# A retention layer and two feed-forward layers on one core: the first block's x made chunk by chunk from PSUM, weight tiles converted one step further ahead, weight loads issued ahead of the stores

## The chip, the core and the metric

The kernel runs on one core of a Trainium2 chip. The metric is the device time of one execution in microseconds (us). Before the change the median of three runs is 888.38 us (887.61 to 889.36). The engines are called as in the profile: PE is TensorE's matrix products (PEld its weight loads), DVE is VectorE, ACT is ScalarE, POOL is GpSimd, SP is the queue that issues most DMAs.

## What is computed

Retention over 4 batches, 8 heads, 576 positions, head size 64, then two feed-forward layers with 2304 tokens, model width 512 and inner width 2048. The weights arrive as 64-bit floats.

```python
scores = (q @ k.T) / sqrt(64)
ret    = scores * Dmat            # gamma_h ** (i - j) for i >= j, else 0
x      = (ret @ v)                # regrouped to 2304 x 512
h = x @ w_in;  x = max(0.01*h, h) @ w_out      # layer 0, leaky
h = x @ w_in2; x = (h * cos(h)) @ w_out2       # layer 1
```

## The kernel before

**Tiles.** The 2304 tokens are 18 chunks of 128 for the retention, and five blocks of 512, 512, 512, 384 and 384 for the feed-forward layers. The inner width is cut into 16 pieces f, so a layer has 5 x 16 steps (block, f) and both layers 160. The retention of chunk i gives the x of 128 tokens; block 0 needs chunks 0 to 3, and these are worked through before the first step. The later chunks are laid between the steps.

**Precision.** Every operand of the feed-forward products is held as a high and a low half (`hi` rounded to fp32r, `lo` the rest), and a product is three fp32r products. So x, the hidden g and the weights w are each split by ACT (the high half) and DVE (the low half: a subtraction). One step has 12 products into the inner width (`h_mm`, L393) and 12 out of it (`o_mm`, L407).

**Weights.** A piece of the weights, here called a grain, comes in as 64-bit words by a DMA (`load_raw`, `load_half`), and is turned into fp32 by `conv_a` (ACT, L307 and L308), `conv_b` (DVE, L313, L315 and L319), `conv_c` (DVE, L326), `conv_d` (ACT, L335, the high half) and `conv_e` (DVE, L338, the low half). The main program calls them as `ready`, `conv_b`, `add_of`, `high_of` and `low_of`. Layer 0's grains are converted while the 16 steps of block 0 run; layer 1's are converted later in halves, each stored to DRAM (`stash`) and fetched again.

**The first x.** For chunk i, `scores` (L166), `masks` (L182), `values` (L197, L211), `states` (L231) and `reads` (L244) leave the chunk's output in two banks of PSUM, and `take` (L270, four ACT instructions of 128x128, one for each of the four groups of heads) scales it into `xr`. Once all four chunks of block 0 are there, `split_x(0)` cuts the four tiles of 128x512 into halves (ACT L379, DVE L380).

**Order.** The schedule is written out by hand: each engine runs its instructions in the order in which the program issues them, and a semaphore wait at the head of an engine's queue holds all behind it. The first part is a list of calls (L572 to L635), then a loop over the steps. In step s of block 0, DVE converts grain s + 2 and makes the low half of grain s + 1, with the low half of g and the work of a later chunk between. SP's DMA issues are in program order too. Before the first chunk the program issues 16 products of zeros (`warm`, L280).

Of the kernel before, what the change touches and what calls it, by code (L numbers as in the profile page):

```python
# [7 lines left out]
F32 = mybir.dt.float32  # L8
F32R = mybir.dt.float32r
# [4 lines left out]
ALU = mybir.AluOpType  # L14
# [5 lines left out]
P = 128  # L20
# [48 lines left out]
def retention_ffn_ffn(  # L69
# [29 lines left out]
        tabs_sb[:, sum(sizes[:x]) : sum(sizes[: x + 1])] for x in range(4)  # L99
    )  # L100

    zero = xp.tile([P, 2 * T], F32, tag="x", name="zero")[:, :P]
    one = const.tile([P, 1], F32, name="one")
    psum = psp.tile([P, 8, 512], F32, name="psum")

# [31 lines left out]
    def scale_v(i):  # L137
        c = i % CYCLE * H
        if i in (1, 2) or n_first <= i < n_busy:
            for h in range(H):  # L140
                v = ch_t[i][:, 3, h * D : (h + 1) * D]
                nc.scalar.activation(v, v, AF.Copy, scale=vtab_sb[:, c + h : c + h + 1])
            return
        v3 = ch_t[i][:, 3].rearrange("p (h d) -> p h d", h=H)
        t3 = vtab_sb[:, c : c + H].unsqueeze(2).to_broadcast([P, H, D])
        eng = nc.gpsimd if i else nc.vector
        eng.tensor_tensor(out=v3, in0=v3, in1=t3, op=ALU.mult)
# [111 lines left out]
    def take(i):  # L259
        b = banks_of(i)  # L260
        j = max(j for j in range(NB) if T0[j] <= i * P)
        t0 = i * P - T0[j]
        c = i % CYCLE
        parts = ((0, 1, c), (1, 2, CYCLE)) if c == CROSS else ((0, 2, c),)
        for p in range(NP):
            if t0 == 0:
                xr[j, p] = xrp.tile([P, T], F32, tag="xr", name="xr")
            o = NP * C + p * C
            for x0, x1, t in parts:
                nc.scalar.activation(  # L270
                    xr[j, p][:, t0 + x0 * C : t0 + x1 * C].rearrange("p (x c) -> p x c", c=C),
                    psum[:, b + x0 : b + x1, o : o + C],
                    AF.Copy,
                    scale=otab_sb[:, t * NP + p : t * NP + p + 1],
                )


    def warm(n, bank):
        for _ in range(n):
            nc.tensor.matmul(psum[:, bank, :P], zero, zero, start=True, stop=True)  # L280

# [39 lines left out]
    def conv_c(g):  # L323
        lo, _ = words(g)
        i = t_t[g].bitcast(I32)
        nc.vector.tensor_tensor(out=i, in0=i, in1=lo.bitcast(I32), op=ALU.add)  # L326
        raw_t.pop(g)
# [18 lines left out]
    def stash_w(g):  # L346
        t = t_t.pop(g)
        both = rawp_t[g].rearrange("p (a n) -> p a n", a=2).bitcast(F32R)
        nc.scalar.copy(both[:, 1], t)  # L349
        nc.gpsimd.tensor_tensor(  # L350
            out=both[:, 0], in0=t, in1=both[:, 1].bitcast(F32), op=ALU.subtract
        )
        nc.sync.dma_start(w2[g[1]][g[2]], rawp_t.pop(g).rearrange("p (a n) -> p a n", a=2))


    def fetch_w(f):
# [148 lines left out]
    def next_half():  # L505
        if half_n[0] < len(half_q):
            load_half(*half_q[half_n[0]])
            half_n[0] += 1
# [7 lines left out]
    def add_of(k):  # L516
        if k < len(grains):
            conv_c(grains[k])
            if grains[k][2] is not None:
                next_half()  # L520
            elif k in after:
                load_raw(after[k])

    def high_of(k):
        if k < len(grains):
            if not grains[k][2]:
                new_w(0, grains[k][1])
            conv_d(grains[k])

    def low_of(k):  # L530
        if k < len(grains):
            conv_e(grains[k], nc.vector)

    def ready(k):
        if k < len(grains):
            conv_a(grains[k])
# [25 lines left out]
    def stash(s):  # L562
        for g in stash_at.get(s - 1, ()):
            conv_b(g)
            conv_c(g)
            stash_w(g)
            next_half()
        for g in stash_at.get(s, ()):
            conv_a(g)

    with tc.manual_schedule():
        nc.scalar.dma_start(tabs_sb, tabs)  # L572
        nc.vector.memset(zero, 0.0)

        nc.scalar.copy(one, zero[:, :1])
        load_chunk(0)
        load_raw(0)
        for i in range(1, n_first):
            load_chunk(i)
        for f in range(1, 4):  # L580
            load_raw(f)
        scale_q(0)
        scale_v(0)
        warm(WARM[0], 3)
        scores(0)
        masks(0)
        ready(0)
        values(0)
        scale_v(1)
        conv_b(grains[0], lambda: scale_q(1))  # L590
        scores(1)
        masks(1)
        values(1)
        scale_v(2)
        states(0)
        reads(0)
        take(0)
        scale_q(2)
        scores(2)
        add_of(0)  # L600
        high_of(0)
        scale_q(3)
        scores(3)
        masks(2)
        ready(1)
        scale_v(3)
        values(2)
        low_of(0)
        masks(3)
        states(1)  # L610
        reads(1)
        take(1)
        values(3)

        def second():
            states(2)

        conv_b(grains[1], second)
        reads(2)
        take(2)  # L620
        states(3)
        reads(3)
        take(3)
        load_chunk(4)
        load_raw(4)
        load_chunk(5)
        for f in range(5, 10):
            load_raw(f)
        for _ in range(2):
            next_half()  # L630
        add_of(1)
        split_x(0)
        high_of(1)
        low_of(1)
        ready(2)  # L635

        for s in range(len(steps) + LAG[1]):
            lj, f = steps[s] if s < len(steps) else (None, None)
            i = chunk_at.get(s)
            if lj is not None:  # L640
                nxt = lj + 1 if lj + 1 < 2 * NB else None
                if s == last:
                    early.close()
                    fp = ctx.enter_context(tc.tile_pool(name="fp", bufs=2))
                if f == 2 and nxt is not None and nxt >= NB:
                    load_x(nxt)
                h_mm(lj, f)
                if f == NF - 1 and nxt is not None and nxt < NB:
                    split_x(nxt)
                if i is not None:  # L650
                    values(i)
                if s + 1 in chunk_at:
                    scores(chunk_at[s + 1])
            prev = steps[s - 1] if 1 <= s <= len(steps) else None
            if lj is not None and lj < NB:
                leaky(lj, f)
                if s < NF:

                    def between():
                        if s:  # L660
                            low_of(s + 1)
                        if s in (1, 2):
                            g_low(*prev)

                    if s + 2 < len(grains):
                        conv_b(grains[s + 2], between)
                    else:
                        between()
                    add_of(s + 2)
                    ready(s + 3)  # L670
                    high_of(s + 2)
                g_high(lj, f)
            if i is not None:
                states(i)
            if s + 1 in chunk_at:
                masks(chunk_at[s + 1])
            if n_first <= chunk_at.get(s + 2, 0) < n_busy:
                scale_q(chunk_at[s + 2])
                scale_v(chunk_at[s + 2])
            if prev and prev[0] < NB and prev in graw:  # L680
                g_low(*prev)
            for q in outs.get(s, ()):
                o_mm(*q)
            if i is not None:
                reads(i)
                take(i)
                if i + 2 < NCH:
                    load_chunk(i + 2)
                    if i + 2 >= n_busy:
                        scale_q(i + 2)  # L690
                        scale_v(i + 2)
            for q in outs.get(s, ()):
                if q[1] == NF - 1:
                    if lj is not None and lj < NB:

                        g_low(lj, f)
                    evacuate(q[0])
            if lj is not None and lj >= NB:
                cos_a(lj, f)
            if prev and prev[0] >= NB:  # L700
                cos_c(*prev)
            if lj is not None and lj >= NB:
                cos_b(lj, f)
            if prev and prev[0] >= NB:
                g_low(*prev)
            stash(s)
            for qj, qf in outs.get(s - 1, ()):
                if qj == NB - 1:
                    fetch_w(qf)
# [49 lines left out]
```

## Time and profile before

| | before |
|---|---|
| median of three runs | 888.38 us |
| the profiled execution's own time | 888.93 us |
| its span (first to last instruction) | 887.1 us |
| busy in the span: PE, DVE, ACT, POOL | 863.2, 575.2, 398.1, 71.2 us |
| mean granted TensorE clock | 0.988 |
| moved by DMA | 110.88 MB |

The 1.8 us between the span and the execution's own time lie around the first and the last instruction. Busy time of a row is the sum over its instructions; a bracket at a row's end gives how long the engine had stood idle before it and what ended that. [...]

### The profile page before, as it was taken

What the parts mean: (1) busy time and instruction counts of PE and PEld (TensorE: products, weight loads), DVE (VectorE), ACT (ScalarE), POOL (GpSimd) and SP (SyncE); (2) the same over time, 40 slices, a digit from 0 to 9 for tenths busy, and PEclk for the clock granted to TensorE, in tenths of its full rate; (3) what the DMA queues carried; (4) which work ended last, traced back from release to release, by engine and by line L of the source; (5) the groups of instructions that cost most, each with busy time, mean ns of one, the idle gap of its engine ahead of it and who ended that gap; (6) DMA issues with size and microseconds to landing.
All of it is one profiled execution on the core that took longest, in us unless ns stands there. A gap on an engine that the chain in (4) does not pass through costs nothing.

```text
span 887.1 us, 14814 instructions
## 1 busy us (share of the span) xinstructions
PE 863.2 (97%) x6048; PEld 753.2 (85%) x6048; DVE 575.2 (65%) x953; ACT 398.1 (45%) x738; POOL 71.2 (8%) x57
## 2 busy tenths in 40 slices
PE   6689999999999999989999999999999999999998
PEld 6568888777887888989999888888888888999998
DVE  5699974343654446554211897777777777888885
ACT  4588764434554446344322343343334333433433
POOL 0000020222212231311000000000000000000000
PEclk8699999999999999999999999999999999999999
DMA  9915522455464546551687700210021002100100
GB/s 361 419 45 198 182 98 83 156 189 168 167 236 144 191 143 215 193 189 71 241 310 261 255 24 1 95 49 1 1 71 48 1 1 72 48 1 1 37 1 35
DMA packets 35860, 110.88 MB, mean 125 GB/s; under 512 B 3408, under 2 KB 8528, under 8 KB 31696
## 3 DMA queue, kind: packets, MB, share of 16 engines
q1 hardware_dynamic: 35648, 109.59, 34.6%
q8 instruction: 47, 0.77, 0.4%
q10 hardware_dynamic: 144, 0.35, 0.1%
q14 instruction: 21, 0.17, 0.1%
HBM read 79.00 MB, written 30.93 MB: 124 GB/s over the span
## 4 chain that ended last, share of the span: by engine, by line
PE 90%; DVE 4%; DMA 3%; ACT 1%; issue 1%; POOL 0%; SPq 0%; DVEq 0%; ACTq 0%; POOLq 0%
PE psum L393 42%; PE psum L407 42%; PE psum L244 2%; DMA raw<-in_w 2%; PE psum L166 1%; PE psum L197 1%; PE psum L211 1%; DVE t L326 1%; DVE t L319 1%; DMA x<-x_hi 1%; ACT t L307 0%; DVE w L338 0%; DVE t L313 0%; DVE g L459 0%; DVE t L315 0%
## 5 line engine op out<-in xcount | busy, mean ns | idle before, releaser
L393 PE MATMUL psum<-x_sb,w 128*128 128x512 f32 (+1 forms) x1920 | 425.3, 370 | 4.8 <-DVE x_sb L380 3.2
L407 PE MATMUL psum<-g,w 128*128 128x512 f32 (+1 forms) x1920 | 424.1, 369 | 0.0
L393 PEld LDWEIGHTS psum<-x_sb,w 128*128 128x128 f32 x1920 | 351.2, 189 | 52.5 <-DVE x_sb L380 3.8
L407 PEld LDWEIGHTS psum<-g,w 128*128 128x128 f32 x1920 | 347.9, 188 | 46.7 <-DVE g L459 0.4
L454 ACT CAST g<-graw 128x512 fp32r<-128x512 f32 (+1 forms) x160 | 92.6, 579 | 221.2 <-DVE graw L483 103.3
L459 DVE TENSOR_TENSOR g<-graw,g 128x512 fp32r<-128x512 f32 (+1 forms) x160 | 103.6, 648 | 86.5 <-ACT g L454 86.3
L477 ACT ACTIVATE r_sb<-r_sb 128x512 f32<-128x512 f32 (+1 forms) x80 | 47.3, 591 | 131.6 <-DVE r_sb L476 131.4
L467 DVE TENSOR_SCALAR t_sb<-psum 128x512 f32<-128x512 f32 (+1 forms) x80 | 51.0, 637 | 63.0 <-PE psum L393 63.0
L445 ACT ACTIVATE graw<-psum 128x512 f32<-128x512 f32 (+1 forms) x80 | 44.2, 553 | 53.6 <-PE psum L393 53.5
L307 ACT ACTIVATE t<-raw 128x512 f32<-128x512 f32 (+1 forms) x49 | 40.1, 819 | 34.4 <-DMA raw<-in_w 32.6
L350 POOL TENSOR_TENSOR t<-t 128x512 fp32r<-128x512 f32 x32 | 43.6, 1368 | 131.1 <-ACT t L349 99.6
L475 DVE SCALAR_TENSOR_TENSOR r_sb<-t_sb,r_sb 128x512 f32<-128x512 f32 (+1 forms) x80 | 51.1, 639 | 2.8
L476 DVE SCALAR_TENSOR_TENSOR r_sb<-t_sb,r_sb 128x512 f32<-128x512 f32 (+1 forms) x80 | 51.1, 639 | 2.7
L474 DVE SCALAR_TENSOR_TENSOR r_sb<-t_sb,psum 128x512 f32<-128x512 f32 (+1 forms) x80 | 50.8, 635 | 2.7
L483 DVE SCALAR_TENSOR_TENSOR graw<-r_sb,psum 128x512 f32<-128x512 f32 (+1 forms) x80 | 50.0, 624 | 1.7 <-ACT r_sb L478 1.7
L478 ACT ACTIVATE r_sb<-r_sb 128x512 f32<-128x512 f32 (+1 forms) x80 | 47.1, 589 | 2.5
L326 DVE CUSTOM_DVE_ANT_0 t<-raw,t 128x1024 uint16<-128x1024 uint16 (+1 forms) x49 | 42.6, 870 | 4.8
L313 DVE TENSOR_SCALAR t<-t 128x512 f32<-128x512 f32 (+1 forms) x49 | 28.1, 574 | 25.6 <-ACT t L307 25.5
L319 DVE SCALAR_TENSOR_TENSOR t<-raw,t 128x512 uint32<-128x512 uint32 (+1 forms) x49 | 42.9, 875 | 1.1
L182 DVE TENSOR_TENSOR p_sb<-psum,tabs_sb 128x512 f32<-128x512 f32 x18 | 12.4, 688 | 47.7 <-PE psum L166 42.6
L308 ACT ACTIVATE raw<-raw 128x512 int32<-128x512 uint32 (+1 forms) x49 | 40.1, 819 | 0.0
L472 DVE TENSOR_SCALAR t_sb<-t_sb 128x512 f32<-128x512 f32 (+1 forms) x80 | 31.5, 393 | 0.0
(35 smaller groups left out, 352.8 us busy)
## 6 DMA issues: line engine op xcount, KB each, us to landing
ch<-in_qkv SPq DMA_DIRECT2D x17, 1024.0 KB, 5.7
raw<-in_w SPq DMA_DIRECT2D x34, 512.0 KB, 5.1
w<-t SPq DMA_DIRECT2D x32, 512.0 KB, 3.0
w<-w SPq DMA_DIRECT2D x32, 512.0 KB, 5.4
raw<-in_w SPq DMA_DIRECT2D x15, 1024.0 KB, 8.8
x_sb<-x SPq DMA_DIRECT2D x12, 512.0 KB, 6.3
x<-x_hi SPq DMA_DIRECT2D x12, 256.0 KB, 2.8
x<-x_lo SPq DMA_DIRECT2D x12, 256.0 KB, 2.9
```

Of the source, the lines that this page charges most:

```text
L319: nc.vector.scalar_tensor_tensor(out=u, in0=hi, scalar=0xC0000000, in1=u, op0=ALU.bitwise_and, op1=ALU.bitwise_or)
L326: nc.vector.tensor_tensor(out=i, in0=i, in1=lo.bitcast(I32), op=ALU.add)
L393: nc.tensor.matmul(hp, wt[:, i ^ hi, ks], x_t[lj, k][:, j, :n], start=(k == 0 and a == 0), stop=(k == KK - 1 and a == 2),)
L407: nc.tensor.matmul(psum[:, BANK_O + m, :n], wt[:, i ^ hi, ms], gt[:, j, :n], start=(f == 0 and a == 0), stop=(f == NF - 1 and a == 2),)
L454: nc.scalar.copy(g_t[lj, f][:, 0, : TB[lj % NB]], g)
L459: nc.vector.tensor_tensor(out=gt[:, 1, :n], in0=graw.pop((lj, f)), in1=gt[:, 0, :n].bitcast(F32), op=ALU.subtract)
L467: nc.vector.tensor_scalar(t, h_t[lj, f], INV_2PI, MAGIC, op0=ALU.mult, op1=ALU.add)
L474: nc.vector.scalar_tensor_tensor(out=r, in0=t, scalar=-C1, in1=hp, op0=ALU.mult, op1=ALU.add)
L475: nc.vector.scalar_tensor_tensor(out=r, in0=t, scalar=-C2, in1=r, op0=ALU.mult, op1=ALU.add)
L476: nc.vector.scalar_tensor_tensor(out=r, in0=t, scalar=-C3, in1=r, op0=ALU.mult, op1=ALU.add)
L477: nc.scalar.activation(r, r, AF.Sin, scale=0.5)
L483: nc.vector.scalar_tensor_tensor(out=g, in0=sq_t.pop((lj, f)), scalar=0.5, in1=h_t.pop((lj, f)), op0=ALU.subtract, op1=ALU.mult,)
```

## The change

Four edits. (1) For block 0 `take` no longer writes `xr`: for each of the four groups of heads ACT writes the high half of the chunk straight from PSUM into the x tile (new L275), and DVE the low half from the same PSUM values (new L276, scale and subtract in one instruction); `split_x(0)` goes. (2) `warm` can issue products of 512 zero columns: two after `values(0)`, two after `reads(3)`; the tile of zeros moves to another buffer. (3) The conversions of block 0 run one grain further ahead: `conv_b` of grains 1 and 2 is issued in the first part, and step s converts grain s + 3 and makes the low half of grain s + 2. (4) In `stash` the next raw load is issued ahead of the store of the grain just converted.

```diff
-    zero = xp.tile([P, 2 * T], F32, tag="x", name="zero")[:, :P]
+    zero = wp.tile([P, T], F32, tag=f"w{NF // 4 - 1}", name="zero")
...
         parts = ((0, 1, c), (1, 2, CYCLE)) if c == CROSS else ((0, 2, c),)
+        if j == 0:
+
+            for p in range(NP):
+                if t0 == 0:
+                    x_t[0, p] = xp.tile([P, 2, T], F32R, tag="x", name="x_sb")
+                hi, lo = (
+                    x_t[0, p][:, e, t0 : t0 + P].rearrange("p (x c) -> p x c", c=C) for e in range(2)
+                )
+                o = NP * C + p * C
+                src, by = psum[:, b : b + 2, o : o + C], otab_sb[:, c * NP + p : c * NP + p + 1]
+                nc.scalar.activation(hi, src, AF.Copy, scale=by)
+                nc.vector.scalar_tensor_tensor(
+                    out=lo, in0=src, scalar=by, in1=hi.bitcast(F32), op0=ALU.mult, op1=ALU.subtract
+                )
+            return
...
-    def warm(n, bank):
+    def warm(n, bank, cols=P):
         for _ in range(n):
-            nc.tensor.matmul(psum[:, bank, :P], zero, zero, start=True, stop=True)
+            nc.tensor.matmul(psum[:, bank, :cols], zero[:, :P], zero[:, :cols], start=True, stop=True)
...
         for g in stash_at.get(s - 1, ()):
             conv_b(g)
             conv_c(g)
+            next_half()
             stash_w(g)
-            next_half()
...
         values(0)
+        warm(2, 1, T)
         scale_v(1)
...
         reads(0)
-        take(0)
         scale_q(2)
         scores(2)
         add_of(0)
+        take(0)
         high_of(0)
...
         reads(1)
+        values(3)
+        conv_b(grains[1], lambda: states(2))
         take(1)
-        values(3)
-
-        def second():
-            states(2)
-
-        conv_b(grains[1], second)
+        ready(2)
         reads(2)
-        take(2)
-        states(3)
+        add_of(1)
+
+        def third():
+            states(3)
+            take(2)
+
+        conv_b(grains[2], third)
+        high_of(1)
         reads(3)
+        warm(2, 7, T)
+        low_of(1)
         take(3)
...
-        add_of(1)
-        split_x(0)
-        high_of(1)
-        low_of(1)
-        ready(2)
+        add_of(2)
+        high_of(2)
+        ready(3)
...
                     def between():
-                        if s:
-                            low_of(s + 1)
                         if s in (1, 2):
                             g_low(*prev)
-
-                    if s + 2 < len(grains):
-                        conv_b(grains[s + 2], between)
+                        low_of(s + 2)
+
+                    if s + 3 < len(grains):
+                        conv_b(grains[s + 3], between)
                     else:
                         between()
-                    add_of(s + 2)
-                    ready(s + 3)
-                    high_of(s + 2)
+                    add_of(s + 3)
+                    ready(s + 4)
+                    high_of(s + 3)
```

What this does to the order on ACT in the first part, from the first `take` to the second (`psum` holds the chunk's output, `w_338` and `w_344` are the first weight tile, `t_` and `raw` the next grain). Before:

```order
L270 ACTIVATE xr<-psum,tabs_sb 128x128 [waits DVE_49,PE_49]
L270 ACTIVATE xr<-psum,tabs_sb 128x128 x3
L335 CAST w_338<-t_195 128x1024 [waits DVE_49]
L307 ACTIVATE t_359<-raw 128x1024 [waits DMAHW7_49]
L308 ACTIVATE raw<-raw 128x1024
```

And now:

```order
L275 ACTIVATE x_sb<-psum,tabs_sb 128x128 [waits DVE_49,PE_49]
L275 ACTIVATE x_sb<-psum,tabs_sb 128x128 [waits DVE_49] x3
L350 CAST w_344<-t_195 128x1024
L322 ACTIVATE t_365<-raw 128x1024 [waits DMAHW7_49]
L323 ACTIVATE raw<-raw 128x1024
```

The second, third and fourth read of a chunk now each wait for DVE, where none waited before.

On DVE, from the third chunk's states to the low half of the third weight tile (`w_565`, now `w_556`; `t_359`, now `t_365`, is grain 1, `t_541`, now `t_471`, is grain 2). Before:

```order
L231 TENSOR_TENSOR st<-psum,st 128x256 [waits DVE_49,PE_49] x2
L326 ISA t_359<-raw,t_359 128x2048 [waits Activation_49]
L380 TENSOR_TENSOR x_sb<-xr,x_sb 128x512 [waits Activation_49] x4
L338 TENSOR_TENSOR w_538<-t_359,w_538 128x1024 [waits Activation_49]
L313 TENSOR_SCALAR t_541<-t_541 128x1024 [waits Activation_49]
L315 TENSOR_SCALAR t_541<-t_541 128x1024 [waits DVE_49]
L319 SCALAR_TENSOR_TENSOR t_541<-raw,t_541 128x1024 [waits DMAHW0_49,DVE_49]
L326 ISA t_541<-raw,t_541 128x2048 [waits DVE_49,Activation_49]
L313 TENSOR_SCALAR t_562<-t_562 128x1024 [waits Activation_49]
L315 TENSOR_SCALAR t_562<-t_562 128x1024 [waits DVE_49]
L338 TENSOR_TENSOR w_565<-t_541,w_565 128x1024 [waits Activation_49]
```

And now:

```order
L231 TENSOR_TENSOR st<-psum,st 128x256 [waits PE_49]
L231 TENSOR_TENSOR st<-psum,st 128x256 [waits DVE_49,PE_49]
L276 SCALAR_TENSOR_TENSOR x_sb<-psum,tabs_sb,x_sb 128x128 [waits Activation_49] x4
L334 SCALAR_TENSOR_TENSOR t_471<-raw,t_471 128x1024 [waits DMAHW0_49]
L353 TENSOR_TENSOR w_506<-t_365,w_506 128x1024 [waits Activation_49]
L276 SCALAR_TENSOR_TENSOR x_sb<-psum,tabs_sb,x_sb 128x128 [waits Activation_49] x4
L341 ISA t_471<-raw,t_471 128x2048 [waits DVE_49]
L328 TENSOR_SCALAR t_558<-t_558 128x1024 [waits DVE_49,Activation_49]
L330 TENSOR_SCALAR t_558<-t_558 128x1024 [waits DVE_49]
L353 TENSOR_TENSOR w_556<-t_471,w_556 128x1024
```

Each chunk's four low halves stand among the conversions, and the last chunk's stand behind the low half of the second weight tile.

On DVE, from the low half of the second step's g (L459, now L475) to the scaling of chunk 4's q (L135), which `scores(4)` on PE waits for. Before, it follows the words of grain 4 (`t_589`):

```order
L459 TENSOR_TENSOR g<-graw,g 128x512 [waits Activation_49]
L319 SCALAR_TENSOR_TENSOR t_589<-raw,t_589 128x1024 [waits DMAHW3_49,DVE_49]
L326 ISA t_589<-raw,t_589 128x2048 [waits DVE_49]
L135 TENSOR_TENSOR ch<-ch,tabs_sb 128x512 [waits DMAHW2_49]
L313 TENSOR_SCALAR t_616<-t_616 128x1024 [waits Activation_49]
```

And now it follows the words of grain 5 (`t_607`):

```order
L475 TENSOR_TENSOR g<-graw,g 128x512 [waits Activation_49]
L353 TENSOR_TENSOR w_610<-t_580,w_610 128x1024
L334 SCALAR_TENSOR_TENSOR t_607<-raw,t_607 128x1024 [waits DMAHW5_49,DVE_49]
L341 ISA t_607<-raw,t_607 128x2048 [waits DVE_49]
L135 TENSOR_TENSOR ch<-ch,tabs_sb 128x512 [waits DMAHW2_49]
L328 TENSOR_SCALAR t_634<-t_634 128x1024 [waits Activation_49]
```

One whole grain more stands ahead of it.

## Rows read from the trace of the kernel before

**Rows 1.** Timeline of PE: start, busy, engine, line, operation, [idle before].

```profile
1.05 6.60 PE L280 MATMUL psum<-zero 128*128 128x128 f32 x32 [1.05 <-DVE zero L573]
...
35.38 8.36 PE L393 MATMUL psum<-x_sb,w 128*128 128x512 f32 x24 [2.48 <-DVE x_sb L380]
...
45.82 2.81 PE L393 MATMUL psum<-x_sb,w 128*128 128x512 f32 x11 [0.76 <-DVE w L338]
48.47 2.88 PE L407 MATMUL psum<-g,w 128*128 128x512 f32 x12
...
54.88 0.69 PE L166 MATMUL psum<-ch 64*64 64x64 f32 x32 [0.81 <-DVE ch L135]
...
66.13 0.68 PE L244 MATMUL psum<-ch,st 64*64 64x64 f32 x16 [0.84 <-DVE st L229]
```

**Rows 2.** Stretches: length, busy us of each engine (instructions), clock, DMA share, GB/s.

```profile
0.00:35.38 35.38, 22.21 (x529) 20.90 (x529) 18.43 (x29) 16.61 (x42) 1.68 (x5) 0.79 0.96 382
35.38:45.82 10.44, 8.86 (x25) 6.52 (x25) 9.39 (x12) 8.51 (x12) 0.00 (x0) 0.73 1.01 418
```

**Rows 3.** Timeline of DVE and ACT in the first part.

```profile
18.59 1.14 ACT L270 ACTIVATE xr<-psum,tabs_sb 128x128 f32<-128x128 f32 x4 [0.44 <-PE psum L244]
18.63 0.69 DVE L135 TENSOR_TENSOR ch<-ch,tabs_sb 128x512 f32<-128x512 f32 x1 [0.54 <-DMA ch<-in_qkv]
...
34.63 2.50 DVE L380 TENSOR_TENSOR x_sb<-xr,x_sb 128x512 fp32r<-128x512 f32 x4 [2.63 <-ACT x_sb L379]
...
44.54 1.23 DVE L338 TENSOR_TENSOR w<-t,w 128x1024 fp32r<-128x1024 f32 x1 [0.54 <-ACT w L335]
```

**Rows 4.** Groups by shape: busy us, mean ns of one | idle before.

```profile
L454 ACT CAST g<-graw 128x512 fp32r<-128x512 f32 x96 | 59.7, 622 | 144.3 <-DVE graw L483 70.6 <-PE psum L407 56.9 <-issue 9.0
...
L270 ACT ACTIVATE xr<-psum,tabs_sb 128x128 f32<-128x128 f32 x64 | 18.3, 369 | 12.8 <-PE psum L244 12.8
...
L307 ACT ACTIVATE t<-raw 128x1024 f32<-128x1024 f32 x15 | 17.2, 1147 | 10.0 <-DMA raw<-in_w 8.2 <-DVE w L338 1.8
...
L335 ACT CAST w<-t 128x1024 fp32r<-128x1024 f32 x15 | 15.8, 1055 | 3.2 <-DVE t L326 3.2
...
L231 DVE TENSOR_TENSOR st<-psum,st 128x256 f32<-128x256 f32 x28 | 11.8, 423 | 27.3 <-PE psum L211 22.8 <-PE psum L244 3.3
...
L573 DVE MEMSET zero<- 128x128 f32 x1 | 0.2, 165 | 0.8 <-PEq L748 0.8
```

**Rows 5.** Timeline of DVE: one grain's conversion while block 0's steps run.

```profile
54.14 0.68 DVE L135 TENSOR_TENSOR ch<-ch,tabs_sb 128x512 f32<-128x512 f32 x1
...
60.80 0.68 DVE L313 TENSOR_SCALAR t<-t 128x1024 f32<-128x1024 f32 x1
...
62.13 1.22 DVE L338 TENSOR_TENSOR w<-t,w 128x1024 fp32r<-128x1024 f32 x1
63.27 1.22 DVE L319 SCALAR_TENSOR_TENSOR t<-raw,t 128x1024 uint32<-128x1024 uint32 x1
64.52 1.23 DVE L326 CUSTOM_DVE_ANT_0 t<-raw,t 128x2048 uint16<-128x2048 uint16 x1
65.66 0.41 DVE L229 COPY st<-psum 128x256 f32<-128x256 f32 x1
66.00 0.68 DVE L459 TENSOR_TENSOR g<-graw,g 128x512 fp32r<-128x512 f32 x1
66.59 0.68 DVE L313 TENSOR_SCALAR t<-t 128x1024 f32<-128x1024 f32 x1
```

**Rows 6.** Timeline of SP, PE and DVE: a raw load and two late waits.

```profile
328.39 0.38 SPq L294 DMA_DIRECT2D raw<-in_w  x1
...
335.56 2.37 PE L393 MATMUL psum<-x_sb,w 128*128 128x384 f32 x12 [0.74 <-DVE x_sb L380]
...
380.66 0.43 DVE L313 TENSOR_SCALAR t<-t 128x512 f32<-128x512 f32 x1 [5.91 <-ACT t L307]
...
384.02 1.15 PE L244 MATMUL psum<-ch,st 64*64 64x64 f32 x32 [3.06 <-DVE st L231]
```

More of the change, by code (lines that the diff above doesn't have):

```diff
@@ L352, in stash_w @@
         )
-        nc.sync.dma_start(w2[g[1]][g[2]], rawp_t.pop(g).rearrange("p (a n) -> p a n", a=2))
+        both = rawp_t.pop(g).rearrange("p (a n) -> p a n", a=2)
+        nc.sync.dma_start(w2[g[1]][g[2]], both)
     def fetch_w(f):
```

## The prediction

> **What bounds the kernel now.** I read the timeline of PE first, since PE is busy 97% of the span and every idle stretch of it is time lost. It stands still for more than half a microsecond at few places [rows 1]: up to 35.38, where the first of block 0's products waits for x; ahead of 45.82, for the low half of the third weight tile; ahead of 54.88, for chunk 4's q, scaled by DVE; ahead of 66.13, for chunk 4's state, also from DVE. After that come only two late waits, 0.74 us at 335.56 and 3.06 at 384.02 [rows 6]. Then I read the stretches [rows 2]: up to 35.38 DVE works 18.43 us of 35.38, from 35.38 to 45.82 it works 9.39 of 10.44. So DVE has room before the first product and none after it. Last I read DVE's own timeline from there [rows 5]: grain after grain without a gap, until PE's backlog hides it from 66.13 on. What the change does to the time is therefore what it does to DVE's arrival at 66.13, and to the two late waits. PE's work after 66.13 is the same in both kernels.
>
> **Prices on DVE** [rows 5], from one start to the next: L313 with L315 1.33 (60.80 to 62.13), L338 1.14, L319 1.25 where L326 follows and 1.14 where something else does, L326 1.14. A grain is thus 4.86 us. A 128x512 operation takes 0.60, a pair of L231 0.85 (two of 423 ns, [rows 4]). From DVE's end to PE's start there is some 0.05 (44.54 + 1.23 to 45.82, [rows 1, 3]); I take this for each handoff between ACT and DVE.
>
> **x from PSUM.** Removed: four ACT casts and four DVE subtractions of 128x512, the latter 2.50 us at 34.63, and the 2.63 that DVE waits ahead of them [rows 3]. Added: 16 small DVE instructions of 128x128 (L276), four a chunk. The order on ACT shows that the second, third and fourth high half of a chunk wait for DVE: the two engines take turns, and DVE waits in line for each turn with all that stands behind it. ACT's half is 369 ns [rows 4], as before. L276 is not in the trace. Above it stands the 128x256 addition from PSUM, 423 ns; below it the 128x128 memset, 165 ns [rows 4]. Length 512 costs 0.68 and 256 costs 0.42, so 128 lies near 0.29, which I take. A pair is 0.37 + 0.29 + 2 x 0.05 = 0.76, and a chunk holds DVE for 3 x 0.76 + 0.2 = 2.5 us even where its first high half is ready.
>
> [...]
>
> **One grain further ahead.** No work is added, but what the engines wait for stands behind one more grain, 4.86 us, as the order on DVE shows for L135. Where DVE has room this is free; I lay DVE's rows in their new order and see where it has none.
>
> Take 0: ACT begins at 18.59 [rows 3], DVE's first half at 19.0, the fourth is through at 21.5. Chunk 3's L135, at 18.63 before, stands behind it: 2.9 us late, and with it PE's scores of chunk 3. Then come L135, two L182, L338, two pairs of L231, L328 with L330, L334: 3 x 0.60 + 1.14 + 2 x 0.85 + 1.33 + 1.14 = 7.1, to 28.6. Take 1 to 31.1; L341 1.14, the next pair of conversions 1.33, chunk 3's states 0.85: 34.4. Take 2 to 36.9; L334 and the second tile's L353, 2.28: 39.2. Now take 3's first half lands: the first product at 39.6 instead of 35.38. Take 3 to 41.7, L341 to 42.95. Here DVE waits: ACT makes the third tile's high half first (1.05) and only then grain 3's words (1.15, [rows 4]), so DVE goes on at 45.2. Two conversions 1.33, the third tile's low half 1.23: 47.8 against 45.77 [rows 3]. PE, ready by about then (24 products took 8.36 us from their start, [rows 1]), is 2.0 late.
>
> Next L334 and L341 follow the low half (started at 46.5): 1.14 + 1.25 + 1.14 = 50.05, L328 and L330 to 51.4, but the first low half of g waits for ACT's high half, behind the fourth tile's: 50.1 + 1.05 + 0.62 [rows 4] = 51.9. The first products out (48.47 before) start at 52.6, 4.1 late. Then 0.60, 1.14, 1.25, 1.14, 1.33 to 57.35, again 0.5 of waiting for ACT, 0.60, and with the fifth tile's low half 1.14, 1.25, 1.14 to 62.0: only here is chunk 4's L135, 0.74 to PE's start. Scores of chunk 4 at 62.75 instead of 54.88: **7.9 us late**. From L135 to L229 DVE has the same kinds of work as before, 11.52 us [rows 5], so 66.13 becomes 74.0, 7.9 late too. After that PE has its backlog, as before.
>
> **Zero products.** [...] They can raise the clock of the first 24 products, whose mean was 0.73 [rows 2], but these end at the third tile's time anyway: worth nothing. The other way, PE now stands idle for nearly 5 us ahead of 62.75, and if its clock falls there, it pays once more what the first 24 products paid at a mean clock of 0.73: 8.36 less twice the 2.88 of the twelve at 48.47 [rows 1], 2.6. The wait of 0.84 that PE had ahead of 66.13 hides that much of it, so 0 to +1.8; I take 0.
>
> **Load ahead of the store.** At 380.66 DVE had waited 5.91 us for ACT, and ACT for a raw load; chunk 13's states stand behind it on DVE, and PE waits 3.06 for them. At 335.56 ACT stood behind such a load with the high half of x: 0.74 [rows 6]. The load stood on SP behind a store that waits for POOL. Now it is behind the store of one grain earlier only, issued some 5 us sooner, and it lands in time. I take both waits away, -3.8; the bounds are 0 and -3.8.
>
> **Sum.** 888.93, the profiled execution's own time, + 7.9 - 3.8 = 893.0; it stands 0.55 above the median of the runs, so **892.5 us**. L276's bounds move it by 16 x 0.13 = 2.1 either way, the clock by up to +1.8: 890.4 to 896.4.
>
> **Rivals.** *The late waits stay* (a load still late, or a new wait behind POOL): 892.5 + 3.8 = 896.3. For it: POOL's work is unchanged and the next store still blocks SP. Against: one grain of slack is over 5 us. *The turns overlap*: if DVE's half runs beside ACT's next, a chunk takes 1.14 [rows 3] + 0.33 instead of 2.96 from ACT's first start, 4 x 1.5 = 6.0 less: 886.5. Against it stand the waits in the order. *DVE uses its room* (the faster side): it works half of the time up to 35.38, so the 16 halves and grain 2 fit there and PE runs without a gap from 35.4 at full clock; it decides if take 3's halves reach DVE before 34. Saved: 2.6 of clock, 2.1 ahead of 45.82 (from 35.38 + 8.36), 0.8 and 0.8 at 54.88 and 66.13, and 3.8, together 10.1: 878. Against it: the room lies in waits for PE and DMA, and in-order takes cannot move into it. *Short halves*: L276 near 0.17 and other slack: 889 to 890, no difference.
>
> **Chances.** Forecast 0.67; late waits stay 0.11; overlap 0.08; room used 0.05; short halves 0.09. About 0.2% (1.8 us) is what a measurement can tell: faster 0.13, same 0.10, slower 0.77. The range is 888.0 to 896.8: below it lie two rivals with 0.13.
>
> **What would show it.** After: the first L409 near 39.6, four L276 a chunk spaced by about 0.76, each waiting for ACT; L166 of chunk 4 near 62.7 after a wait for L135; L244 near 74; no waits of PE from there to the end but around the block changes. Wrong: L276s back to back, or a first L409 before 36; or PE waiting 3 us near 390 again.

## The result, and the profile after

The changed kernel took **893.47 us** (median of four runs, 892.64 to 893.85), the kernel before beside it 888.48 (887.61 to 889.36, four runs): a ratio of 1.0052 [1.0036, 1.0068], slower by 5.0 us. The prediction was 892.5, in a range of 888.0 to 896.8. The profiled execution of the changed kernel took 892.64, its span is 890.9 and its mean granted clock 0.989. It is the shortest of its kernel's four runs, while that of before (888.93) lies 0.55 above its kernel's median, so the traces differ by 3.8 us where the medians differ by 5.0.

The timeline of PE after (start, busy, engine, line, operation, [idle before]) answers [rows 1]:

```profile
10.23 1.98 PE L295 MATMUL psum<-zero 128*128 128x512 f32 x4
...
36.24 3.50 PE L295 MATMUL psum<-zero 128*128 128x512 f32 x4
39.48 6.07 PE L409 MATMUL psum<-x_sb,w 128*128 128x512 f32 x24
...
47.66 2.81 PE L409 MATMUL psum<-x_sb,w 128*128 128x512 f32 x11 [0.58 <-DVE w L353]
52.48 4.61 PE L423 MATMUL psum<-g,w 128*128 128x512 f32 x12 [2.01 <-DVE g L475]
...
62.47 0.69 PE L166 MATMUL psum<-ch 64*64 64x64 f32 x32 [2.64 <-DVE ch L135]
63.10 4.61 PE L423 MATMUL psum<-g,w 128*128 128x512 f32 x12
...
74.40 0.68 PE L244 MATMUL psum<-ch,st 64*64 64x64 f32 x16
```

Five places that stood at 35.38, 45.82, 48.47, 54.88 and 66.13 now stand at 39.48, 47.66, 52.48, 62.47 and 74.40: late by 4.1, 1.8, 4.0, 7.6 and 8.3 us. Three of these places wait for DVE. The first stands behind the second pair of zero products, but comes no later than DVE lets it: x's first low half from chunk 3 was through at 39.43. The last stands behind slow products: the twelve behind 63.10 took 4.61 us, in a stretch whose granted clock was 0.66, where twelve behind 71.45 took 3.02, in one whose clock was 1.00.

The stretches between them (length, busy us of PE, PEld, DVE, ACT and POOL with instructions, clock, DMA share, GB/s) answer [rows 2]:

```profile
0.00:39.48 39.48, 25.09 (x536) 20.46 (x536) 25.40 (x44) 18.30 (x40) 1.25 (x5) 0.83 0.93 371
...
62.47:67.54 5.07, 5.07 (x44) 4.06 (x45) 5.00 (x6) 5.07 (x13) 0.00 (x0) 0.66 0.00 0
...
74.40:890.90 816.50, 812.97 (x5345) 711.13 (x5344) 524.18 (x885) 352.36 (x658) 67.48 (x52) 1.00 0.32 112
```

The last one is the gain: from chunk 4's state to the end the kernel before took 887.1 - 66.13 = 820.97, now it takes 816.50. PE's waits of 0.74 and 3.06 [rows 6] are gone, and it has no other wait there. So 8.3 are lost early, 4.5 are given back late, and the span grows by 3.8.

Where the early loss begins, on ACT and DVE at the first chunk's x, against [rows 3]:

```profile
18.18 0.37 ACT L275 ACTIVATE x_sb<-psum,tabs_sb 128x128 fp32r<-128x128 f32 x1
18.97 0.37 ACT L275 ACTIVATE x_sb<-psum,tabs_sb 128x128 fp32r<-128x128 f32 x1 [0.42 <-DVE x_sb L276]
...
18.58 0.35 DVE L276 SCALAR_TENSOR_TENSOR x_sb<-psum,tabs_sb,x_sb 128x128 fp32r<-128x128 f32 x1 [0.56 <-ACT x_sb L275]
19.37 0.35 DVE L276 SCALAR_TENSOR_TENSOR x_sb<-psum,tabs_sb,x_sb 128x128 fp32r<-128x128 f32 x1 [0.44 <-ACT x_sb L275]
...
21.20 0.68 DVE L135 TENSOR_TENSOR ch<-ch,tabs_sb 128x512 f32<-128x512 f32 x1
```

ACT's second half starts only when DVE's first is through, and DVE's second only when ACT's is: from one to the next 0.79 us, of which either engine works less than half. L135, at 18.63 before, stands behind all four, at 21.20.

### The profile page after: what moved, and what is told of

It is laid out like the page before. It is cut to its first block, busy times and chain, and to the rows that moved or that the text cites. A ratio compares the mean times of both kernels' runs of the same rounds, so it can differ in the third digit from the quotient of the medians.

```text
span 890.9 us, 14845 instructions
## 1 busy us (share of the span) xinstructions
PE 866.7 (97%) x6056; PEld 752.8 (85%) x6056; DVE 580.1 (65%) x965; ACT 397.4 (45%) x734; POOL 68.7 (8%) x57
## 4 chain that ended last, share of the span: by engine, by line
PE 93%; DVE 0%; issue 0%; ACT 0%
PE psum L423 45%; PE psum L409 43%; PE psum L244 2%; PE psum L166 1%; PE psum L197 1%; PE psum L211 1%; DVE t L341 0%; DVE w L353 0%; DVE t L334 0%; DVE ch L135 0%; ACT o_sb L438 0%; DVE g L475 0%
## 5 line engine op out<-in xcount | busy, mean ns | idle before, releaser
L475 DVE TENSOR_TENSOR g<-graw,g 128x512 fp32r<-128x512 f32 (+1 forms) x160 | 104.4, 653 | 94.7 <-ACT g L470 94.6
```

The costliest lines, as they stand in the source:

```text
L475: nc.vector.tensor_tensor(out=gt[:, 1, :n], in0=graw.pop((lj, f)), in1=gt[:, 0, :n].bitcast(F32), op=ALU.subtract)
```

## The experiments

Two sets of four, each on one chip with the kernel before beside it: 890.48 there (888.97 to 893.93, 18 runs) for the first four, 889.59 (886.34 to 891.52, 15 runs) for the others. Ratios are to these, with 95% intervals. The kernel before ran 1 to 2 us slower on these chips than beside the changed kernel, for a reason that no run shows, so differences between kernels are read from spans and from places in the trace. The changed kernel was not run again beside them. "L244 of chunk 4" is the place that stood at 66.13 before and 74.40 after; its line number differs by a few between kernels.

**1. The load ahead of the store alone** (the kernel before with edit 4):

```diff
             conv_c(g)
-            stash_w(g)
             next_half()
+            stash_w(g)
```

> The kernel before with the fourth edit alone: the raw load issued ahead of the store. Theory: the late gain of the changed kernel, 4.5 us between chunk 4's L244 and the end (820.97 to 816.5), is this edit's, so 888.5 - 4.5 = 884.0, with no wait of PE left near 335 and 384. Rival: the late gain comes from the conversions ending a step sooner, or from PE running later against the DMAs; then this is 888.5 and the waits of 0.7 and 3.1 us stay.

Measured: 883.60 us, ratio 0.9923 [0.9907, 0.9939], span 881.8. Its timeline of PE, and its last stretch:

```profile
34.98 7.83 PE L393 MATMUL psum<-x_sb,w 128*128 128x512 f32 x24 [2.47 <-DVE x_sb L380]
...
54.82 0.70 PE L166 MATMUL psum<-ch 64*64 64x64 f32 x32
...
65.37 0.68 PE L244 MATMUL psum<-ch,st 64*64 64x64 f32 x16
```

```profile
65.37:881.80 816.43, 812.97 (x5344) 711.36 (x5344) 529.37 (x891) 355.83 (x661) 67.45 (x52) 1.00 0.32 113
```

Up to L244 its program is that of the kernel before, yet in this execution DVE reached chunk 4's L135 0.8 us sooner (53.38 against 54.14), and L244 came 0.8 sooner, without its wait. By so much the early part of two executions of the same instructions can differ; it is no gain of the edit. From there to the end it takes 816.43, as in the changed kernel: 4.5 us gained late, 5.3 in the span. This version is faster than both kernels.

**2. The changed kernel with the store ahead again** (edit 4 undone):

```diff
-            next_half()
             stash_w(g)
+            next_half()
```

> The changed kernel with its fourth edit undone: store first, then load. Theory: the loss up to chunk 4's L244 stays at 8.3 us and the late waits come back, 893.5 + 4.5 = 898.0, or 0.7 to 1 less if only the two waits of 0.74 and 3.06 return. Rival (the late gain is not the load's): 893.5.

Measured: 899.07, ratio 1.0099 [1.0078, 1.0121], span 898.8. PE's late waits are back:

```profile
345.16 2.35 PE L409 MATMUL psum<-x_sb,w 128*128 128x384 f32 x12 [1.97 <-DVE x_sb L396]
...
367.21 0.69 PE L197 MATMUL psum<-p_sb,ch 64*64 64x64 f32 x32 [0.52 <-DVE p_sb L182]
...
394.20 1.15 PE L244 MATMUL psum<-ch,st 64*64 64x64 f32 x32 [3.27 <-DVE st L231]
395.28 3.88 PE L409 MATMUL psum<-x_sb,w 128*128 128x384 f32 x12
398.99 2.24 PE L423 MATMUL psum<-g,w 128*128 128x384 f32 x12
```

They are 5.8 us together, and the twelve products behind the longest take 3.88 where the next twelve take 2.24. From chunk 4's L244, at 74.51, to the end it is 824.29, 7.8 more than in the changed kernel; this profiled run, of 900.61, lies 1.5 above the median of its kernel. Experiments 1 and 2 show from both sides that the late gain is the order of the two DMAs on SP.

**3. x by way of `xr` again, one grain ahead kept** (the changed kernel with edit 1 undone):

```diff
-        if j == 0:
...
-            return
...
+        split_x(0)
         add_of(2)
```

> The changed kernel with its first edit undone: x goes by xr and split_x(0) again, while the conversions stay one grain further ahead, the zero products and the load order stay. Theory: without the turns DVE gets through its rows sooner. Its order up to chunk 4's L135 then holds the four subtractions (2.5 us) instead of four takes of 2.6 us and the waits about them, so scores of chunk 4 near 58 instead of 62.5 and chunk 4's L244 near 69.5, 3.5 later than before and 5 earlier than in the changed kernel: 888.5 + 3.5 - 4.5 = 887.5. That it stays later than before is the price of the extra grain ahead of L135. Rival (the extra grain alone loses the time): 893.5. Rival (a grain ahead is worth its 4.9 us): about 880.

Measured: 887.43, ratio 0.9965 [0.9952, 0.9978], span 885.6. Its PE around chunk 4, and DVE's copy that L244 waits for:

```profile
56.22 1.14 PE L166 MATMUL psum<-ch 64*64 64x64 f32 x32 [4.22 <-DVE ch L135]
57.28 5.11 PE L408 MATMUL psum<-g,w 128*128 128x512 f32 x12
...
69.11 0.68 PE L244 MATMUL psum<-ch,st 64*64 64x64 f32 x16
```

```profile
67.00 0.42 DVE L229 COPY st<-psum 128x256 f32<-128x256 f32 x1
```

Without edit 1 the span is 5.3 us shorter. Against experiment 1 it is still 3.7 us late at L244. Of these 2.0 are DVE's, whose data are there at 67.42; the other 1.7 are PE's own: behind the wait of 4.22 twelve products take 5.11, in a stretch whose granted clock was 0.55. So the 69.5 that was expected came out in part by luck: DVE was 2 us sooner than laid out (scores of chunk 4 at 56.22, not 58), and the clock, which the expectation left out, gave most of it back.

**4. The same x from PSUM, without the turns** (per chunk four high halves on ACT, then four low halves on DVE):

```diff
+            parts = []
             for p in range(NP):
...
                 nc.scalar.activation(hi, src, AF.Copy, scale=by)
+                parts.append((hi, lo, src, by))
+            for hi, lo, src, by in parts:
                 nc.vector.scalar_tensor_tensor(
```

> The changed kernel with the turns taken out of take: ACT makes the four high halves of a chunk first, then DVE its four low halves; the instructions and all else stay. Theory (DVE's waiting in the turns costs, not its 16 instructions): a chunk holds DVE for some 1.1 to 1.4 us instead of 2.6, so 5 to 5.5 us less up to chunk 4's L244 (69.0 to 69.5): 888 to 888.5. Rival (the 16 instructions' own time, 5.6 us against 2.5, is the cost): no more than 1 us less, 892.5 to 893.5.

Measured: 887.71, ratio 0.9967 [0.9954, 0.9980], span 885.3. DVE's low halves of the first chunk, and PE:

```profile
18.85 1.13 DVE L279 SCALAR_TENSOR_TENSOR x_sb<-psum,tabs_sb,x_sb 128x128 fp32r<-128x128 f32 x4 [0.78 <-ACT x_sb L276]
19.89 0.69 DVE L135 TENSOR_TENSOR ch<-ch,tabs_sb 128x512 f32<-128x512 f32 x1
```

```profile
36.14 9.32 PE L412 MATMUL psum<-x_sb,w 128*128 128x512 f32 x36
...
68.86 0.68 PE L244 MATMUL psum<-ch,st 64*64 64x64 f32 x16
```

The four halves now hold DVE for 1.04 (18.85 to 19.89) where the turns held it for 2.62 (18.58 to 21.20), and the banks are still read by one engine at a time. PE is at chunk 4's L244 5.5 us earlier, as early as without edit 1 (69.11 in experiment 3): all that edit 1 costs in the changed kernel lies in the turns.

**5. Without the wide zero products:**

```diff
-        warm(2, 1, T)
...
-        warm(2, 7, T)
```

> The changed kernel without its two pairs of zero products of 512 columns. Theory: they lie in waits and neither cost nor give anything; the first product stays at 39.2 to 39.5, chunk 4's L244 at 74.4, and the time within 0.7 us of the changed kernel (893.5). Rival 1: the second pair delays the first products and with them all that follows; then 1 to 2 us faster. Rival 2: the pairs hold the clock of the first 24 products up; then these take 1 us or more longer, and the time is 1 to 2 us longer if that shows at the end.

Measured: 893.86, ratio 1.0036 [1.0023, 1.0050], against 1.0052 [1.0036, 1.0068] for the changed kernel: no difference that the times can tell. In the traces it is 1.2 longer, 892.1 against 890.9.

```profile
39.87 10.98 PE L409 MATMUL psum<-x_sb,w 128*128 128x512 f32 x36 [3.17 <-DVE x_sb L276]
52.89 3.06 PE L423 MATMUL psum<-g,w 128*128 128x512 f32 x12 [2.04 <-DVE g L475]
...
63.95 4.98 PE L423 MATMUL psum<-g,w 128*128 128x512 f32 x12
...
75.62 0.68 PE L244 MATMUL psum<-ch,st 64*64 64x64 f32 x16
```

The first products are not sooner without the zeros, since they wait for DVE. They are slower: 36 take 10.98 at a granted clock of 0.80, where the 24 of the changed kernel took 6.07 in a stretch whose clock was 1.00 (39.48 to 47.66). But they still end before the wait at 52.89, which is as long in both (2.04 and 2.01). L244, expected at 74.4, came at 75.62 though DVE's L229 had started at 73.67: again slow products stand ahead of it (4.98 for the twelve behind 63.95, where the twelve behind 72.67 took 3.02).

**6. The turns without the extra grain** (the changed kernel with the first part and the steps in the order of before):

```diff
-                        low_of(s + 2)
-                    if s + 3 < len(grains):
-                        conv_b(grains[s + 3], between)
+                    if s + 2 < len(grains):
+                        conv_b(grains[s + 2], between)
```

> The changed kernel with its turns, its zero products and the load ahead of the store, but with the first tiles converted only as far ahead as before. Theory: the turns alone still hold DVE up, and without the extra grain chunk 4's words come a grain earlier; but what the turns cost now comes ahead of the first product. I lay DVE's rows in this order and get the first product near 41.5, chunk 4's L166 at 60.5 to 61, its L244 at 71.9, and with the 816.4 us that every kernel with the load ahead took from there to the end: a span of 888.3, a time of 890.1. Rival, the two prices simply add: 893.5 less the 3.8 by which the extra grain without turns (887.4) lay above the load ahead alone (883.6): 889.7, L244 at 70.6. Rival, only the turns cost: no change against 893.5, L244 at 74.4.

Measured: 891.13, ratio 1.0017 [1.0005, 1.0029], span 889.8.

```profile
39.83 3.78 PE L295 MATMUL psum<-zero 128*128 128x512 f32 x4
42.62 6.83 PE L409 MATMUL psum<-x_sb,w 128*128 128x512 f32 x24
...
62.07 0.69 PE L166 MATMUL psum<-ch 64*64 64x64 f32 x32 [0.81 <-DVE ch L135]
...
73.32 0.68 PE L244 MATMUL psum<-ch,st 64*64 64x64 f32 x16 [0.83 <-DVE st L229]
```

Every place is 1.1 to 1.6 us later than expected. The first product stands behind the zero products here, for x's first low half was through at 40.70; L166 and L244 wait for DVE. Only 1.1 us of L244's delay go with the extra grain, not the 3.7 of experiment 3 against 1. By the medians it is 2.3 (893.47 less 891.13, not run side by side) against 3.8: the prices do not add.

**7. The load ahead, and two low halves on POOL** (experiment 1, meant to be better still):

```diff
-            conv_e(grains[k], nc.vector)
+            conv_e(grains[k], nc.gpsimd if k in (2,3) else nc.vector)
```

> A version meant to beat both: the kernel before with the raw load issued ahead of the store, and the low halves (word less high half) of block 0's grains 2 and 3 computed on POOL, which has nothing to do until 72 us, and no longer on DVE, which is the late one. Theory: DVE is 2.3 us ahead at chunk 4's L135, PE's waits ahead of L166 and L244 of chunk 4 (0.8 each before) go, the third tile's low half comes 0.2 us later from POOL; chunk 4's L244 at 64.7, span 881.1, time 882.5 to 883 against 883.6. Rival: POOL's subtraction of 128x1024 takes so much longer than DVE's 1.23, or slows DVE so much on the way, that PE waits for the third tile instead: 884 to 886.

Measured: 885.99, ratio 0.9947 [0.9934, 0.9960], against 0.9923 [0.9907, 0.9939] for experiment 1; L244 of chunk 4 is at 67.94 against 65.37: the rival was right. POOL, DVE and PE:

```profile
44.22 2.35 POOL L338 TENSOR_TENSOR w<-t,w 128x1024 fp32r<-128x1024 f32 x1 [24.41 <-ACT w L335]
...
44.69 2.41 DVE L459 TENSOR_TENSOR g<-graw,g 128x512 fp32r<-128x512 f32 x1 [1.06 <-ACT g L454]
47.03 1.21 DVE L319 SCALAR_TENSOR_TENSOR t<-raw,t 128x1024 uint32<-128x1024 uint32 x1
...
46.62 4.36 PE L393 MATMUL psum<-x_sb,w 128*128 128x512 f32 x11 [1.92 <-POOL w L338]
```

POOL needs 2.35 for what DVE does in 1.23, so the third tile is late; and DVE's own subtraction, 0.68 elsewhere, takes 2.41 beside it and ends 0.53 after POOL's. What DVE was to save it spends in its two subtractions beside POOL's (2.41, and 2.50 at 51.14): its L135 of chunk 4 starts at 55.95, against 53.38 in experiment 1.

**8. Neither turns nor extra grain** (experiment 6 with the edit of experiment 4):

```diff
+                parts.append((hi, lo, src, by))
+            for hi, lo, src, by in parts:
                 nc.vector.scalar_tensor_tensor(
```

> The changed kernel with neither the turns (the four high halves on ACT, then the four low ones on DVE) nor the extra grain ahead: x straight from PSUM, zero products and the load ahead of the store remain. Theory: with DVE's rows in this order the first product comes near 39.1, because x's last low halves stand on DVE behind grain 1's words; L244 of chunk 4 at 68.6, span 885.1, time 886.9: no better than with the extra grain (887.7), 3 us over the load ahead alone (883.6). Rival, the prices simply add (x from PSUM without turns cost 0.3: 887.7 against 887.4): 883.9, L244 at 65.7.

Measured: 887.28, ratio 0.9966 [0.9953, 0.9978], span 884.8, L244 at 68.35: as expected, and not where the prices would add up. DVE's waits for the halves of chunk 0 and of chunk 3, and the stretch up to the first product, here and then in experiment 4:

```profile
18.75 1.12 DVE L279 SCALAR_TENSOR_TENSOR x_sb<-psum,tabs_sb,x_sb 128x128 fp32r<-128x128 f32 x4 [1.18 <-ACT x_sb L276]
...
36.96 1.13 DVE L279 SCALAR_TENSOR_TENSOR x_sb<-psum,tabs_sb,x_sb 128x128 fp32r<-128x128 f32 x4 [3.25 <-ACT x_sb L276]
```

```profile
0.00:38.01 38.01, 23.29 (x537) 19.56 (x537) 20.82 (x43) 15.33 (x39) 1.25 (x5) 0.87 0.93 375
```

```profile
0.00:36.14 36.14, 23.80 (x537) 19.61 (x537) 25.66 (x48) 18.35 (x42) 1.25 (x5) 0.87 0.95 382
```

The extra grain puts 4.84 us more of DVE's work ahead of the first product, and that comes 1.9 us sooner (38.01 to 36.14). In experiment 8 DVE stands in line for each chunk's high halves with nothing else to do; the extra grain fills these waits.

**The six together.** Start of DVE's L135 of chunk 4 / start of PE's L244 of chunk 4, us. From L244 to the end all six took 816.43 to 816.50, so this is the whole difference between their spans.

| load ahead of the store in all | no extra grain | one grain further ahead |
|---|---|---|
| x by way of `xr` | 53.38 / 65.37 | 55.48 / 69.11 |
| x from PSUM, four and four | 56.35 / 68.35 | 56.18 / 68.86 |
| x from PSUM, in turns | 61.33 / 73.32 | 61.73 / 74.40 |

Each entry is one trace, and experiment 1 shows that an early part can move by 0.8 with nothing changed. The turns cost 5.0 to 5.5 us in either column. Of the rest, the extra grain alone makes 3.7 at L244, x from PSUM alone 3.0, and both together 3.5, no more than one of them. By DVE's L135, which leaves PE's clock out, it is plainer: the extra grain makes 2.1 by way of `xr`, and with x from PSUM nothing beyond that 0.8 (-0.2 and +0.4): the grain is done in the time in which DVE waits for x.

## Why the prediction was right, step by step

- **DVE is late, PE waits for it.** Right: all five places came within 0.4 us of the forecast (39.6, 47.8, 52.6, 62.75, 74.0), in the order forecast. Three have DVE as the releaser, as named; PE has no wait ahead of the first and the last. DVE's own rows kept to the forecast within half a microsecond too: 28.25 for the second chunk's first half where 28.6 was forecast, 39.08 for 39.2, 61.73 for 62.0.
- **Turns.** Right in kind and size: 0.79 a pair against 0.76. Inside it L276 took 0.35, not 0.29, within its bounds. Experiment 4 takes the turns away and gets 5.5 us back; the rival that they overlap had priced that at 6.0.
- **One grain further ahead.** The prediction gave turns and grain one sum, 7.9 at L244; 8.3 were measured. It can now be split against experiment 1, which stands 0.8 earlier, so that there are 9.0 to split: 3.5 come without the turns (experiment 4) and 5.5 with them. That DVE has room before the first product and none after it is what experiments 4 and 8 show; that an in-order take wastes this room, as was said against the rival of the room used, is seen in experiment 8.
- **Clock.** Mis-sized: taken as 0 in bounds of 0 to +1.8, it cost 0.7. DVE's L229 row in the changed kernel, and the twelve products behind L166 in the kernel before:

```profile
73.26 0.42 DVE L229 COPY st<-psum 128x256 f32<-128x256 f32 x1
```

```profile
55.51 3.02 PE L407 MATMUL psum<-g,w 128*128 128x512 f32 x12
```

  Its data are there at 73.68, but PE comes only at 74.40 and without a wait, since these twelve, behind 63.10, now took 4.61 at a mean clock of 0.66: 1.6 more, of which the wait that PE had ahead of 66.13 hides a part, as the prediction said. DVE alone would have made it 73.7, where 74.0 was forecast. PE's idle time ahead of 62.47 was 2.64 and not the nearly 5 of the prediction, because the twelve products at 52.48 were slow too (4.61, at a granted clock of 0.63).
- **Zero products.** Worth nothing that the times can tell, as said, and for the reason said: with them the first 24 products run at a higher clock (1.00 from 39.48 to 47.66, against 0.80 for the first 36 without), but the products after these wait for the third tile and for g all the same (experiment 5). The pair at 10.23 took 1.98 us at a granted clock of 1.00, the pair at 36.24 took 3.50, of which the 3.24 up to the first product lie at 0.52.
- **Load ahead of the store.** Right, -4.5 instead of -3.8: the two waits of [rows 6] make 3.8; of the rest 0.5 are busy time of PE (813.51 before, 812.97 after) and 0.1 small gaps. The store, the load behind it and ACT's wait for that load in the kernel before:

```profile
374.35 0.33 SPq L353 DMA_DIRECT2D w<-t  x1
374.77 0.38 SPq L294 DMA_DIRECT2D raw<-in_w  x1
379.96 0.66 ACT L307 ACTIVATE t<-raw 128x512 f32<-128x512 f32 x1 [8.33 <-DMA raw<-in_w]
```

  and the load and the store in the changed kernel:

```profile
373.08 0.33 SPq L309 DMA_DIRECT2D raw<-in_w  x1
377.82 0.33 SPq L369 DMA_DIRECT2D w<-t  x1
```

  At this place the load now leaves 4.7 us ahead of the store, close to the 5 that were forecast, and from 76 us on ACT has no wait for a raw load left, where before it had ten, 24.4 us together. Without edit 4 the changed kernel loses 7.8 in the same stretch (experiment 2), where a third wait and slower products come in. Whether the edit is worth more there than in the kernel before is not shown: by the medians it is 5.6 in the changed kernel (not run side by side) and 6.9 in the kernel before.

The two errors in size, +0.4 at L244 and -0.7 late, turn the 893.0 of the sum into 892.7, and 892.64 was measured. That it fits so closely is luck in part: at L244 DVE was 0.3 early and the clock 0.7 late, and the median of the runs lies 0.8 above the profiled one, so that the medians moved by 5.0 where 4.1 was forecast.

## What to carry to other kernels

Before an in-order engine is made to share work element by element with another, count the handoffs: four and four cost 1.04 us of DVE's queue where four turns cost 2.62, for the same bytes, with the banks read by one engine at a time in both. Work issued earlier is free only where the engine stands idle before the deadline; lay its rows in the new order up to the next instruction that another engine waits for. And time an edit of several parts part by part: here one line, a load ahead of a store that waits, was worth 4.5 us alone in the traces, and the other three together cost 8.3.

## What the runs showed of the hardware

- A DVE subtraction beside one on POOL. A 128x512 subtraction with both operands in SBUF took 2.41 us on DVE beside one of 128x1024 on POOL, 0.68 otherwise (experiment 7); the second pair the same, 2.50 beside POOL's 2.42. POOL's first started at 44.22 and ended at 46.57, and DVE's, from 44.69, ended 0.53 later. In the kernel before, one of 128x384 took 1.25 beside POOL's L350 (at 361.52), 0.56 without it (366.97). What made them longer no run shows.
- The clock after a wait. Behind PE's waits of 2.64 (changed kernel), 3.27 (experiment 2) and 4.22 (experiment 3) the next twelve products took 4.61, 3.88 and 5.11 us, where others of their shape took 2.88, 2.24 and 2.88; the granted clocks were 0.66 from 62.47 to 67.54, 0.86 from 390 to 402 and 0.55 from 56.22 to 62.40. The wait's length alone does not decide: behind 2.01 twelve products took 4.61 in the changed kernel, behind 2.04 they took 3.06 in experiment 5.
- PE stands still in the first part for no reason that the profile shows ("issue"). In the kernel before:

```profile
PE psum L211 <- issue: 2.0, 1, 2.0
PE psum L244 <- issue: 1.9, 1, 1.9
```

  They lie at 21.3 and 27.7, while the DMA engines are busy at a share of 0.96; later, with a share of 0.32, there is none in 820 us. Experiment 1 had two, of 1.6 and 2.7, experiment 6 none. What PE waits for there no run shows.
